# Batch 0's gate and value products: three float32r passes in the last six steps

## Chip, cores and metric

The kernel runs on 1 core of one Trainium2 chip. The metric is the device time of one execution in microseconds (us); lower is better. A core has TensorE (PE, matmuls), VectorE (DVE), ScalarE (ACT), GpSimd (POOL) and SyncE (SP). SP and ACT issue the transfers (DMA) of this kernel. Each engine works through its own list of instructions in the order in which they were written, and semaphores join the lists.

## The reference

Attention in both directions between a sequence `x` and a small `state`, then a gated feed-forward layer, then a second one:

```
scores = (x @ state.T) / sqrt(D);  a  = softmax(scores);  xread = a @ state
scores2 = (state @ x.T) / sqrt(D); a2 = softmax(scores2); sread = a2 @ x
x = concat([xread, sread], axis=2), heads side by side     # 8 batches x 544 rows, 512 columns
g = x @ w_gate;  silu = g * (1 / (1 + exp(-g)));  val = x @ w_val
x = (silu * val) @ w_out                                   # d_ff = 1536
h = x @ w_in2;   g = h * (1 / (1 + exp(-1.702 * h)))
x = g @ w_out2                                             # d_ff = 2048
```

Eight batches, 8 heads, 512 sequence rows, 32 state rows, head width 64.

## The kernel before

**Stages.** The first feed-forward layer runs batch by batch: batch 0 first, then batches 1 to 6, the state rows of all batches, batch 7. The second layer follows. The change touches batch 0 alone (`i == 0` in the code), which lies between about 25 and 154 us of the trace.

**A stage.** It has twelve steps f = 0 to 11, one for each 128 columns of d_ff. In a step PE makes the gate product (`pg`), then the value product (`pv`), and then adds the step before's result `h` into four accumulators (`out1(f - 1)`, 12 float32r passes). Behind each of the three stands a *place*, written (f, 0), (f, 1) and (f, 2), at which a plan puts other work: the next batch's attention, weight work, transfers. The plan is a table by place (`BLOCK0` for batch 1's attention, `plan_weights` for the weights), and what a place holds is written to every engine's list there and then. Nothing is moved later.

**The gate and value products.** xread is not formed. `sw` holds the state times the gate and value weights: for each batch, unit u (two steps) and group of four heads g a tile of 128 x 512 (tag `xo`). A product is the sum over g = 0, 1 of `sw` times the softmax `a` of the group. In batch 0 both are whole float32, and a product is two float32 matmuls (`mm_whole`, L337). In all other batches both are kept as a high and a low float32r part, and a product is six float32r matmuls (`mm_rows`, L330 to L332): high x high, low x high, high x low, for each g.

**Batch 0's weights.** They come whole from HBM: SP loads them (`raw`), ACT takes two passes over them (L203, L204), DVE two (L212, L213), POOL one (L216), together a *decode*. Weights of `w_out` are then also split into float32r parts by ACT (L250) and POOL (L251). A *job* (`quad_job`, PE L629, two halves into two PSUM tiles `at`) multiplies a decoded tile with the states of four batches; ACT copies the first half out (L635) and DVE the second (L636), and at the next place ACT issues their store to HBM (`move`, L652). For u of 2 and more, batch 0's rows of the result are also sent by SP from the copies into `sw`'s `xo` tile (L648). The `at` tiles have two PSUM buffers, so a half of a job waits until the tile that held its buffer before has been copied out.

**Next batch.** At (9, 0) and (9, 1) ACT issues the loads of batch 1's first `sw` rows into two tiles `xf` (`fetch`, L661), and at (10, 0) and (10, 1) `cut_fetched` splits them: ACT writes the high part (L667), POOL the low part (L668). At (9, 2) batch 1's second softmax follows on ACT, with a load of its table ahead (L503); its sums stand on DVE at (10, 0) ahead of that job's copy, and the transposes of its result on PE at (10, 1) (L540).

**Softmax tiles.** `a` of even batches lies in pool `ae`, of odd ones in `ao`.

Of the kernel before, what the change touches and what calls it, by code (L numbers as in the profile page):

```python
# [8 lines left out]
F32 = mybir.dt.float32  # L9
F32R = mybir.dt.float32r  # L10
U32 = mybir.dt.uint32
ACTF = mybir.ActivationFunctionType
ALU = mybir.AluOpType
# [61 lines left out]
def kernel(  # L75
# [24 lines left out]
    B, H, S, D = x.shape  # L100
    NS = state.shape[2]
    DM = H * D
    FF1 = w_gate.shape[1]
    FF2 = w2_in.shape[1]
    P = 128
    KD = DM // P
    F1 = FF1 // P
    U1 = F1 // 2
# [7 lines left out]
    v, a, pe, pool_e, sy = nc.vector, nc.scalar, nc.tensor, nc.gpsimd, nc.sync  # L116
# [4 lines left out]
    work = ctx.enter_context(tc.tile_pool(name="work", bufs=2))  # L121
# [7 lines left out]
    ao = ctx.enter_context(tc.tile_pool(name="odd", bufs=1, side="right"))  # L129
    ae = late.enter_context(tc.tile_pool(name="even", bufs=1, side="right"))  # L130
# [5 lines left out]
    def f32(t):  # L136
        return t.bitcast(F32)
# [147 lines left out]
    def need_whole(key):  # L285
        while pos["done"] <= where[key]:
            before = pos["done"], pos["begun"]
            whole_slot()
            assert before != (pos["done"], pos["begun"]), key
# [44 lines left out]
    def mm_whole(ps, pairs):  # L334

        for k, (w, x_) in enumerate(pairs):
            pe.matmul(ps, w, x_, start=k == 0, stop=k == len(pairs) - 1)  # L337
# [14 lines left out]
    def at():  # L352
        if extra:
            extra.append(extra.pop(0))
            if extra[0] != "at":
                return psa.tile([P, 512], F32, name="at", tag=extra[0])
        return pst.tile([P, 512], F32, name="at", tag="at")
# [43 lines left out]
    class Group:  # L401
# [118 lines left out]
            v.transpose(out=self.aT, in_=self.sp)  # L520

        def a_tile(self):
            return (ae, ao)[self.b % 2].tile([P, 2, S], F32R, name="a", tag=f"a{self.g}")

        def back_full(self):
            self.a = self.a_tile()
# [77 lines left out]
    sw = {}  # L604
# [11 lines left out]
    moved = [[], []]  # L616
    FIRST = {0: 1, 1: 4}
    OWN = 2

    def quad_job(qd, u, k, late=False):  # L620


        if qd == 0:
            need_whole(("gv", u, k))
        w = whole[u * KD + k]
        ps = [at(), at()]
        for hl in range(2):
            r = slice(hl * 64, hl * 64 + 64)
            pe.matmul(ps[hl], quad_t[qd][r, k], w[r], start=True, stop=True)  # L629
        pos["jobs"] += 1  # L630
        if qd == 0 and not late or pos["jobs"] % 3 == 0:
            t = ap.tile([P, 2, DM], F32, name="qs", tag="qs", bufs=2)
        else:
            t = work.tile([P, 2, DM], F32, name="qs", tag="raw", bufs=RAWS)
        a.copy(t[:, 0], ps[0])  # L635
        v.tensor_copy(t[:, 1], ps[1])  # L636
        g, q = divmod(k, 2)
        skip = NS * (1 - qd)
        if q == 0:
            quads[qd, u, g] = dp.tile([4 * (P - skip), DM], F32, name=f"sw{qd}_{u}_{g}")  # L640
        rows = quads[qd, u, g].rearrange("(q h p) m -> q p h m", q=2, h=2)
        moved[qd].append((rows[q], t[skip:]))
        if qd == 0 and u >= OWN:
            if q == 0:
                sw[0, u, g] = x_tiles(xp, u % 2 * 2 + g, DM)
            for hl in range(2):
                r = slice(q * 64 + hl * NS, q * 64 + hl * NS + NS)
                sy.dma_start(f32(sw[0, u, g][0][r]), t[:NS, hl])  # L648

    def move():  # L650
        for to, t in moved.pop(0):
# [3 lines left out]
    fetched = {}  # L655
# [7 lines left out]
    def cut_fetched(b, u, g, home=None):  # L663
        t = fetched.pop((b, u, g))
        pl, tag = home or (xp, f"x{u % 2 * 2 + g}")
        x_ = pl.tile([P, 2, DM], F32R, name="xo", tag=tag)
        a.copy(x_[:, 0], t)  # L667
        pool_e.tensor_tensor(x_[:, 1], t, f32(x_[:, 0]), op=ALU.subtract)  # L668
        sw[b, u, g] = x_[:, 0], x_[:, 1]

    def job_places(b):

        if b == 0:
            own = [-2, 0, 1, 2]
            first = [(n, 0, k) for k, n in enumerate((0, 1, 2, 3))]
            last = [(n, 1, k) for k, n in enumerate((28, 30, 32, 34))]
            return [(n, 0, u, k) for n, u, k in first + last] + [
                (6 * (u - 1) + own[k], 0, u, k) for u in range(OWN, U1) for k in range(KD)
            ]
        if b < 4:  # L680
            return [(n, 1, *divmod(8 * (b - 1) + j, KD)) for j, n in enumerate((3, 6, 9, 15, 18, 21, 30, 33))]
        return []

    def plan_weights(plan, i):


        b = order1[i]
        nb = order1[i + 1] if i + 1 < NB1 else None
        if nb == B:
            nb = None  # L690

        def put(f, place, fn, *args):
            plan.setdefault((f, place), []).append(lambda: fn(*args))

        for n, qd, u, k in job_places(b):
            put(n // 3, n % 3, quad_job, qd, u, k, n >= 3 * F1 - 6)
        for g in range(2):
            if 0 < b < B:
                put(b == 1, g, cut_fetched, b, 1, g)
                if b == 1:  # L700
                    put(0, g + 1, fetch, b, 1, g)
                for u in range(2, U1):
                    put(2 * u - 3, g + 1, fetch, b, u, g)
                    put(2 * u - 2 + (b == B - 1), g + (b < B - 1), cut_fetched, b, u, g)
            if nb is not None:
                put(9, g, fetch, nb, 0, g)
                put(10, g, cut_fetched, nb, 0, g, (ae, f"a{g}") if b == B else None)
                if nb > 1:
                    put(11, g, fetch, nb, 1, g)

    def mm_state(ps, b, f, t):

        c = slice(t * 2 * P + f % 2 * P, t * 2 * P + f % 2 * P + P)
        pairs = []
        if b == 0:
            mm_whole(ps, [(f32(sw[b, f // 2, g][0])[:, c], f32(groups[b, g].a[:, 0])) for g in range(2)])
            return
        for g in range(2):
            wh, wl = sw[b, f // 2, g]
            at_ = groups[b, g].a  # L720
            pairs.append((wh[:, c], wl[:, c], at_[:, 0], at_[:, 1]))
        mm_rows(ps, pairs)

# [5 lines left out]
    groups = {}  # L729
# [34 lines left out]
    def add_gv(u, k):  # L764
        r, c = slice(k * P, (k + 1) * P), slice(u * 2 * P, (u + 1) * 2 * P)
        add(("gv", u, k), (w_gate[r, c], w_val[r, c]), "place")

    for u in range(OWN):
        for k in range(KD):
            add_gv(u, k)  # L770
    for f in range(F1):
        if f // 2 + OWN < U1:
            for k in range(2):
                add_gv(f // 2 + OWN, f % 2 * 2 + k)
        add(("o", 0, f), src_out(w_out, f), "place", w1o)
# [24 lines left out]
    def x_tiles(pl, k, N):  # L800
        t = pl.tile([P, 2, S], F32R, name="xo", tag=f"x{k}")
        return t[:, 0, :N], t[:, 1, :N]
# [98 lines left out]
    for i, blk in enumerate(order1):  # L901
# [69 lines left out]
        for f in range(F1):  # L971
# [8 lines left out]
            run(f, 0)  # L980
            if i == 0 and f % 2 == 1 and f // 2 + 1 < OWN:
                state_weights(f // 2 + 1, 1)
# [348 lines left out]
```

## Time and profile before

| | us |
|---|---|
| median of 3 runs | 1491.13 |
| lowest and highest run | 1490.16 and 1491.84 |
| the profiled execution | 1492.28 |
| its span, first to last instruction | 1490.5 |
| PE busy in the span | 1467.6 (98%) |
| DVE, ACT, POOL busy | 915.6, 684.2, 396.1 |
| batch 0's steps 6 to 11 in the trace | 95.30 to 154.36 |

A row of a timeline gives the start of an instruction, its busy time, the engine, the line, the operation with its tiles (out<-in), its shape, and how many records were merged. A bracket at the end tells how long the engine had been idle before it, and what released it. A float32 matmul leaves two records. Busy times of matmuls overlap, so the length of a piece of PE's work is read from its start to the start of what follows it.

### The profile page before, as it was taken

Reading aid. Unit: us, or ns where it says so; the run is one execution under the profiler, and the core shown is the slowest. Engines: PE = TensorE matmul, PEld = TensorE weight load, DVE = VectorE, ACT = ScalarE, POOL = GpSimd, SP = SyncE. Lnnn points to the kernel's source line nnn. Section 1 sums busy time; section 2 is a strip of 40 time slices with the busy share of each in tenths; the row PEclk is TensorE's granted clock in tenths of the full one; section 3 lists DMA queues with packets and bytes.
Section 4 is the critical chain, followed back from the end, with each engine's and each line's share of the span. In section 5 each row is a group of like instructions: output and inputs, shape, how many; then the busy total and the mean of one; then the engine's idle time right before and its main releaser. Section 6 shows DMA issues by size and latency. Waiting matters only on the chain.

```text
span 1490.5 us, 21226 instructions
## 1 busy us (share of the span) xinstructions
PE 1467.6 (98%) x7688; PEld 1193.8 (80%) x7688; DVE 915.6 (61%) x1600; ACT 684.2 (46%) x1247; POOL 396.1 (27%) x325
## 2 busy tenths in 40 slices
PE   7999999999999999999999999999999999999998
PEld 4445677777787777898788889999999999999997
DVE  7985565656678787943344335656565665656554
ACT  6766554555566666654444333333333232323322
POOL 2665221222234445477646330000000000000000
PEclk9999999999999999999999999999999999999999
DMA  7975433333365656425657746565654646574653
GB/s 217 292 248 159 133 99 110 108 125 105 126 189 172 197 170 190 130 100 171 207 189 270 261 147 211 180 232 174 209 198 170 240 159 240 178 240 165 207 183 128
DMA packets 138480, 269.30 MB, mean 181 GB/s; under 512 B 46728, under 2 KB 57992, under 8 KB 138376
## 3 DMA queue, kind: packets, MB, share of 16 engines
q1 hardware_dynamic: 114680, 223.64, 45.5%
q10 hardware_dynamic: 23696, 44.31, 8.9%
q8 instruction: 61, 1.00, 0.3%
q14 instruction: 43, 0.35, 0.1%
HBM read 202.11 MB, written 63.70 MB: 178 GB/s over the span
## 4 chain that ended last, share of the span: by engine, by line
PE 84%; DMA 5%; DVE 4%; ACT 3%; issue 2%; POOL 1%; SPq 0%; ACTq 0%; DVEq 0%; POOLq 0%
PE acc L340 8%; PE acc L341 8%; PE acc L342 8%; PE acc L952 5%; PE acc L954 5%; PE gv L330 5%; PE acc L953 5%; PE gv L331 4%; PE gv L332 4%; DMA xf<-sw 4%; PE gv L1232 4%; PE gv L1231 4%; PE gv L1230 4%; PE at L629 4%; PE at L1230 3%; PE at L1231 3%
## 5 line engine op out<-in xcount | busy, mean ns | idle before, releaser
L798 DVE TENSOR_TENSOR h<-sg,h 128x512 fp32r<-128x512 f32 (+1 forms) x240 | 193.5, 806 | 129.8 <-ACT h L797 128.2
L797 ACT CAST h<-sg 128x512 fp32r<-128x512 f32 (+1 forms) x251 | 149.8, 597 | 170.4 <-DVE sg L1264 80.2
L340 PE MATMUL acc<-wo,h 128*128 128x512 f32 x512 | 200.6, 392 | 0.0
L341 PE MATMUL acc<-wo,h 128*128 128x512 f32 x512 | 200.6, 392 | 0.0
L342 PE MATMUL acc<-wo,h 128*128 128x512 f32 x512 | 199.2, 389 | 0.0
L1254 ACT ACTIVATE sg<-wt 128x512 f32<-128x512 f32 x56 | 35.4, 632 | 299.5 <-DVE wt L1252 299.5
L668 POOL TENSOR_TENSOR xo<-xf,xo 128x512 fp32r<-128x512 f32 x84 | 110.9, 1325 | 231.9 <-ACT xo L667 216.5
L952 PE MATMUL acc<-h,wu 128*128 128x512 f32 (+1 forms) x428 | 165.9, 388 | 0.1
L954 PE MATMUL acc<-h,wu 128*128 128x512 f32 (+1 forms) x428 | 163.8, 383 | 2.0 <-DVE h L798 2.0
L953 PE MATMUL acc<-h,wu 128*128 128x512 f32 (+1 forms) x428 | 163.4, 382 | 0.0
L330 PE MATMUL gv<-a,xo 128*128 128x512 f32 x336 | 137.3, 409 | 0.0
L331 PE MATMUL gv<-a,xo 128*128 128x512 f32 x336 | 133.9, 399 | 0.6 <-POOL xo L668 0.5
L332 PE MATMUL gv<-a,xo 128*128 128x512 f32 x336 | 133.0, 396 | 0.0
L992 DVE TENSOR_TENSOR sg<-gv,sg 128x512 f32<-128x512 f32 (+1 forms) x107 | 70.5, 659 | 83.1 <-PE gv L332 50.7
L342 PEld LDWEIGHTS acc<-wo,h 128*128 128x128 f32 x512 | 96.2, 188 | 20.8
L340 PEld LDWEIGHTS acc<-wo,h 128*128 128x128 f32 x512 | 96.6, 189 | 17.1
L341 PEld LDWEIGHTS acc<-wo,h 128*128 128x128 f32 x512 | 96.6, 189 | 15.8
L1252 DVE TENSOR_TENSOR wt<-wt,gv 128x256 f32<-128x256 f32 x56 | 23.6, 421 | 136.4 <-PE gv L1232 136.4
L952 PEld LDWEIGHTS acc<-h,wu 128*128 128x128 f32 x428 | 80.9, 189 | 22.1 <-issue 6.1
L977 ACT ACTIVATE sg<-gv 128x512 f32<-128x512 f32 (+1 forms) x108 | 61.5, 570 | 80.1 <-PE gv L332 77.0
L954 PEld LDWEIGHTS acc<-h,wu 128*128 128x128 f32 x428 | 80.9, 189 | 21.1 <-DVE h L798 5.5
L1232 PE MATMUL gv<-xo,wu 128*128 128x256 f32 x336 | 95.4, 284 | 0.0
(178 smaller groups left out, 3438.6 us busy)
## 6 DMA issues: line engine op xcount, KB each, us to landing
wo<-w2b SPq DMA_DIRECT2D x128, 512.0 KB
wc<-w2c SPq DMA_DIRECT2D x84, 512.0 KB
xf<-sw ACTq DMA_DIRECT2D x84, 256.0 KB
raw<-in_moe_w_out_dram SPq DMA_DIRECT2D x28, 512.0 KB
sw<-qs ACTq DMA_DIRECT2D x24, 512.0 KB
sw<-qs ACTq DMA_DIRECT2D x24, 384.0 KB
xn<-in_x_dram SPq DMA_DIRECT2D x16, 512.0 KB
y<-ev SPq DMA_DIRECT2D x16, 512.0 KB
```

Of the source, the lines that this page charges most:

```text
L330: pe.matmul(ps, wh, xh, start=k == 0, stop=False)
L331: pe.matmul(ps, wl, xh, start=False, stop=False)
L332: pe.matmul(ps, wh, xl, start=False, stop=k == len(pairs) - 1)
L340: pe.matmul(ps, lh, rh, start=first, stop=False)
L341: pe.matmul(ps, lh, rl, start=False, stop=False)
L342: pe.matmul(ps, ll, rh, start=False, stop=last)
L797: a.copy(h_, src)
L798: eng.tensor_tensor(l_, src, f32(h_), op=ALU.subtract)
L952: pe.matmul(ps, w[:, 0, c], h[:, 0, :N], start=f == 0, stop=False)
L953: pe.matmul(ps, w[:, 1, c], h[:, 0, :N], start=False, stop=False)
L954: pe.matmul(ps, w[:, 0, c], h[:, 1, :N], start=False, stop=f == F1 - 1)
L1232: pe.matmul(ps, w[:, 0, c], x_[:, 1, kt], start=False, stop=kt == 1)
```

## The change

`OWN3 = 3` is new. Batch 0's products of units 3, 4 and 5, which are the steps 6 to 11, go through `mm_rows`; units 0 to 2 stay with `mm_whole`. For that:

- `a` of batch 0 is written into `ao`, and `cut_own` splits it at (4, 0) for g = 0 and at (4, 2) for g = 1 into a tile of `ae`: ACT the high part, DVE the low part.
- Batch 0's rows of units 3 to 5 go by the same transfers into a tile `xf`, and `cut_fetched` splits them into `xo` at (5, 0), (5, 1), (7, 0), (7, 1), (9, 0) and (9, 1).

```
 def a_tile(self):
-    return (ae, ao)[self.b % 2].tile(...)
+    return (ae, ao)[self.b % 2 or not self.b].tile(...)
...
+OWN3 = 3
...
 if qd == 0 and u >= OWN:
-    if q == 0:
+    if q == 0 and u < OWN3:
         sw[0, u, g] = x_tiles(xp, u % 2 * 2 + g, DM)
+    elif q == 0:
+        fetched[0, u, g] = work.tile([P, DM], F32, name="xf", tag="xf", bufs=2)
+    to = fetched[0, u, g] if u >= OWN3 else f32(sw[0, u, g][0])
     for hl in range(2):
...
-        sy.dma_start(f32(sw[0, u, g][0][r]), t[:NS, hl])
+        sy.dma_start(to[r], t[:NS, hl])
...
+def cut_own(g):
+    t = f32(groups[0, g].a[:, 0])
+    own[g] = a_ = ae.tile([P, 2, S], F32R, name="a", tag=f"a{g}")
+    a.copy(a_[:, 0], t)
+    v.tensor_tensor(a_[:, 1], t, f32(a_[:, 0]), op=ALU.subtract)
...
 for g in range(2):
+    if b == 0:
+        put(4, 2 * g, cut_own, g)
+        for u in range(OWN3, U1):
+            put(2 * u - 1, g, cut_fetched, b, u, g)
...
-if b == 0:
+if b == 0 and f // 2 < OWN3:
     mm_whole(...)
...
-    at_ = groups[b, g].a
+    at_ = own[g] if b == 0 else groups[b, g].a
```

On ACT around places (9, 0) to (9, 2) of batch 0, where ST is the scores of batch 1's second group, xf_1148 and xf_1173 are the two fetched tiles, and ACT_TABLE_LOAD stands ahead of the softmax, before:

```order
L462 COPY ST_1146<-at_1143 128x512 [waits PE_49]
L661 DMA xf_1148<-sw0_0_0_373 128x1x512
L250 CAST wu_1153<-wt_1121 128x512 [waits Pool_49]
L635 COPY qs_1169<-at_1165 128x512 [waits DMAHW6_49,DMAHW7_49,DMAHW0_49,PE_49]
L661 DMA xf_1173<-sw0_0_1_440 128x1x512
L797 CAST h_1156<-sg_1140 128x512 [waits DVE_49]
L203 ACTIVATE wt_1189<-raw_1042 128x512 [waits DMAHW2_49]
L204 ACTIVATE raw_1042<-raw_1042 128x512
L652 DMA sw0_1_0_1172<-qs_1169 96x2x512 [waits DVE_49,Activation_49]
L503 ACT_TABLE_LOAD
```

The same stretch of ACT after the change; xf_1056 and xf_1143 are batch 0's rows of unit 5:

```order
L462 COPY ST_1192<-at_1189 128x512 [waits PE_49]
L671 CAST xo_1194<-xf_1056 128x512
L665 DMA xf_1197<-sw0_0_0_373 128x1x512 [waits Pool_49]
L250 CAST wu_1206<-wt_1163 128x512
L636 COPY qs_1222<-at_1218 128x512 [waits DMAHW6_49,DMAHW7_49,DMAHW0_49,PE_49]
L671 CAST xo_1226<-xf_1143 128x512 [waits DMAHW2_49,DMAHW1_49]
L665 DMA xf_1229<-sw0_0_1_440 128x1x512 [waits Pool_49]
L813 CAST h_1209<-sg_1186 128x512 [waits DVE_49]
L203 ACTIVATE wt_1245<-raw_1076 128x512
L204 ACTIVATE raw_1076<-raw_1076 128x512
L656 DMA sw0_1_0_1225<-qs_1222 96x2x512 [waits DVE_49]
L503 ACT_TABLE_LOAD
```

Two casts (L671) came in, and both fetches now wait for POOL: a fetched tile takes the buffer that POOL's split of batch 0's rows reads. The high part is cast from the same buffer just ahead of each.

On DVE around places (4, 0) and (4, 1), from the copy of job (4, 0) to the copy of job (4, 1), before:

```order
L636 COPY qs_742<-at_739 128x512
L212 TENSOR_SCALAR wf_711<-wf_711 128x512
L213 SCALAR_TENSOR_TENSOR wf_711<-raw_644,wf_711 128x512
L992 TENSOR_TENSOR sg_736<-gv_747,sg_736 128x512
L511 TENSOR_REDUCE sq_677<-sp_676 128x16
```

The same stretch of DVE after:

```order
L637 COPY qs_742<-at_739 128x512
L681 TENSOR_TENSOR a_747<-a_304,a_747 128x512
L212 TENSOR_SCALAR wf_711<-wf_711 128x512
L213 SCALAR_TENSOR_TENSOR wf_711<-raw_644,wf_711 128x512
L1008 TENSOR_TENSOR sg_736<-gv_750,sg_736 128x512
L511 TENSOR_REDUCE sq_677<-sp_676 128x16
```

The subtraction for the low part of `a` (L681) stands directly behind the job's copy and ahead of the decode; it waits for ACT's cast of the high part.

## Rows read from the trace of the kernel before

**Rows 1.** Page, busy time: engine, us, share of the span, instructions.

```profile
PE 1467.6 (98%) x7688; PEld 1193.8 (80%) x7688; DVE 915.6 (61%) x1600; ACT 684.2 (46%) x1247; POOL 396.1 (27%) x325
```

**Rows 2.** Timeline of PE, steps 6 and 7 of batch 0: float32 products among their neighbours.

```profile
99.53 1.98 PE L337 MATMUL gv<-a,xo 128*128 128x512 f32 x4
101.44 1.13 PE L629 MATMUL at<-wf,qt 64*128 64x512 f32 x4
...
106.51 1.98 PE L337 MATMUL gv<-a,xo 128*128 128x512 f32 x4
108.33 0.60 PE L432 MATMUL at<-ident,xn 128*128 128x128 f32 x4
108.77 1.88 PE L337 MATMUL gv<-a,xo 128*128 128x512 f32 x4
110.58 1.13 PE L629 MATMUL at<-wf,qt 64*128 64x512 f32 x4
```

**Rows 3.** Timeline of PE in batch 1: two six-pass products, first pass and successor.

```profile
160.73 0.48 PE L330 MATMUL gv<-a,xo 128*128 128x512 f32 x1
...
162.30 1.20 PE L629 MATMUL at<-wf,qt 64*128 64x512 f32 x4
163.43 0.50 PE L330 MATMUL gv<-a,xo 128*128 128x512 f32 x1
...
164.94 0.40 PE L452 MATMUL at<-xth,stc 128*128 128x512 f32 x1
```

**Rows 4.** Timeline of DVE in batch 0.

```profile
76.13 0.90 DVE L212 TENSOR_SCALAR wf<-wf 128x512 uint32<-128x512 uint32 x1
...
85.73 0.69 DVE L636 COPY qs<-at 128x512 f32<-128x512 f32 x1 [2.32 <-PE at L629]
...
91.14 1.48 DVE L534 TENSOR_TENSOR a<-aT,a 128x512 fp32r<-128x512 f32 x1
...
97.19 1.17 DVE L575 TENSOR_SCALAR srd<-at,sm 32x64 f32<-32x64 f32 x4
...
138.07 0.69 DVE L636 COPY qs<-at 128x512 f32<-128x512 f32 x1
```

**Rows 5.** Timeline of ACT in batch 0.

```profile
78.32 0.58 ACT L635 COPY qs<-at 128x512 f32<-128x512 f32 x1
...
116.50 0.62 ACT L250 CAST wu<-wt 128x512 fp32r<-128x512 f32 x1 [0.78 <-POOL wt L216]
...
118.63 0.58 ACT L635 COPY qs<-at 128x512 f32<-128x512 f32 x1
...
128.54 0.58 ACT L462 COPY ST<-at 128x512 f32<-128x512 f32 x1 [1.12 <-PE at L337]
128.55 1.11 ACTq L661 DMA_DIRECT2D xf<-sw  x1
...
131.31 0.59 ACT L635 COPY qs<-at 128x512 f32<-128x512 f32 x1 [0.99 <-PE at L629]
131.32 0.53 ACTq L661 DMA_DIRECT2D xf<-sw  x1
...
134.28 1.28 ACT L503 ACT_TABLE_LOAD   x1 [0.64 <-DVE qs L636]
```

**Rows 6.** Timeline of POOL in batch 0: the low part of a fetched tile.

```profile
139.90 1.30 POOL L668 TENSOR_TENSOR xo<-xf,xo 128x512 fp32r<-128x512 f32 x1 [2.96 <-ACT xo L667]
```

**Rows 7.** Timeline of PE in batch 0: halves of jobs, and the transposes at (10, 1).

```profile
98.51 1.09 PE L629 MATMUL at<-wf,qt 64*128 64x512 f32 x2 [0.28 <-DVE srd L575]
...
119.72 1.13 PE L629 MATMUL at<-wf,qt 64*128 64x512 f32 x4
...
138.90 0.63 PE L540 MATMUL at<-ident,e 128*128 128x128 f32 x4
```

**Rows 8.** Windows: stretch, its length, PE, PEld, DVE, ACT, POOL busy, granted clock, DMA share, GB/s.

```profile
78.00:80.00 2.00, 1.05 (x2) 0.29 (x2) 1.97 (x4) 2.00 (x5) 1.31 (x2) 1.00 0.13 45
80.00:84.53 4.53, 4.53 (x13) 3.31 (x12) 3.31 (x6) 2.19 (x5) 2.48 (x3) 0.62 0.89 250
```

More of the change, by code (lines that the diff above doesn't have):

```diff
@@ L522, in a_tile @@
         def a_tile(self):
-            return (ae, ao)[self.b % 2].tile([P, 2, S], F32R, name="a", tag=f"a{self.g}")
+            return (ae, ao)[self.b % 2 or not self.b].tile([P, 2, S], F32R, name="a", tag=f"a{self.g}")
         def back_full(self):
@@ L669, in cut_fetched @@
         sw[b, u, g] = x_[:, 0], x_[:, 1]
+    own = {}
+    def cut_own(g):
[3 more added lines that the diff above has]
+        v.tensor_tensor(a_[:, 1], t, f32(a_[:, 0]), op=ALU.subtract)
     def job_places(b):
```

## The prediction

> **What bounds the kernel now.** The page's busy times come first: PE works 98% of the span [rows 1], so a stage ends when PE has done its list, and the question is what PE's list gets shorter by and where PE begins to wait. In batch 0 the second question is open, because there all engines decode weights beside the products. The timelines of PE, DVE, ACT and POOL between 70 and 155 us answer it place by place. The reader is to see two things in them. A product of batch 0 is read from its start to the start of what follows [rows 2], a six-pass product in batch 1 likewise [rows 3]. And some pieces of PE's list already start at the moment at which a copy on DVE or ACT ends: the second half of job (6, 0) 0.28 us after PE was free [rows 7], and the transposes at (10, 1), which start at 138.90, when the copy that DVE began at 138.07 and that took 0.69 has just ended [rows 4, 7]. At such a place a shorter product before it gains nothing, and anything put in front of the copy costs PE its full length.
>
> **The products.** Twelve change. A float32 product takes 1.91 us between two jobs (99.53 to 101.44), 1.82 after a job and ahead of transposes, 1.81 between transposes and a job [rows 2]. Six float32r passes take 1.57 between transposes and a job, and 1.51 after a job when other full-height work follows [rows 3]; between two jobs I estimate 1.59. Six products (gate of 6, 8, 10; value of 7, 9, 11) save 1.81 - 1.57 = 0.24 each, the value products of 6 and 8 save 0.32, the other four 0.31: 1.44 + 0.64 + 1.24 = 3.3 us, or 0.22%. In order: 1.67 up to the end of value product 8, 0.31 in gate product 9, 0.79 from there to the transposes at (10, 1), 0.55 in step 11.
>
> The Trainium skill, "FP8 and Floating Point Precision", section "TensorE Precision Notes", counts four passes for true FP32. By it a product would go from eight passes to six, and at the 0.235 us a pass of [rows 3] twelve products would give an estimated 5.6 us; the rows show 3.3, since passes that follow a half-height job or stand ahead of one cost more, and the sum goes by the rows.
>
> **What is added.** ACT gets eight casts (two of `a`, six of rows), 0.5 to 0.6 us each; POOL six subtractions of 1.30 [rows 6]; DVE two, each between 0.69 (the length of its plain passes over 128x512 [rows 4]) and 1.48 (the same operation for batch 1's softmax, [rows 4]). DVE's are free only where DVE waits anyway. The transfers are as many and as large as before, into `xf` in place of `xo`; a later fill waits for POOL's split of the tile before, with weight loads behind it on SP, but that split lies a place earlier, and I cost it at nothing. The new home of `a` makes batch 1's cast at (5, 1) wait for a product that PE has then done: nothing.
>
> **First wait, job (6, 0).** In step 4 DVE's subtraction stands ahead of the decode that began at 76.13 [rows 4]. It waits for a cast that on ACT can only follow the job's copy (78.32, 0.58 [rows 5]), so until about 79.4. Everything behind it on DVE starts some 3.9 us later. I estimate that DVE makes this good by 85.73, with the 2.32 us in which it waited for PE there and with passes that ran long beside POOL, as the one at 76.13, and now run alone [rows 4]. PE's job (4, 2) is then not held up. The second subtraction at (4, 2) finds no such gap: ACT's cast, 0.4 us of waiting and 0.65 of work leave DVE about 1.05 us late until step 6, where POOL's extra splits also run against it. The state sums that began at 97.19 [rows 4] then end at about 99.4 in place of 98.36. PE arrives 0.24 earlier and its second half starts at about 99.55 in place of 98.51 [rows 7]. So PE is 1.0 us late there (bounds: 0.2, if DVE catches up, and 1.6, if the second subtraction also takes 1.48).
>
> **Second wait, job (8, 1).** POOL does 2 x 1.30 us more in step 7 [rows 6]; I estimate that between 0.7 and 1.5 of it falls into time in which POOL stood idle. ACT's cast at 116.50 already waits for POOL there (0.78), and the copy at 118.63 stands 2.13 us behind it [rows 5]. POOL 1.1 to 1.9 us later moves that copy to 119.7 to 120.5, with its end at 120.3 to 121.0; the second half of job (8, 1), which before could start half a us after 119.72 [rows 7], waits for it. The products of value 6 to value 8 have by then won back 1.43, which goes into this wait or the first. I take PE 0.3 us late after this job, with ends of -1.67 (no wait at all) and +0.8.
>
> **Third wait, the transposes at (10, 1).** This is the largest term. I count from ACT's copy of the scores, S = 128.54 [rows 5], which follows PE. Before, the fetch is issued at once (1.11 us), the table load starts at 134.28, S + 5.74, and ACT has 0.99 and 0.64 us of slack ahead [rows 5]. Now: cast of unit 5's rows, done at S + 1.1; POOL's split 1.30, S + 2.4; only then may ACT issue the fetch (0.53 to 1.11 us [rows 5]), S + 3.0 to 3.5, and everything behind it on ACT has waited. Cast of `w_out`, job copy and second cast end at S + 4.6 to 5.2, while POOL subtracts the `w_out` tile until S + 4.9 to 5.4 and the second rows until S + 6.2 to 6.8. The second fetch waits for that. Then `h` (0.5) and the decode pair (1.1) follow, and the table load starts at S + 8.4 to 9.0, 2.7 to 3.3 us late. Behind it stand the exponentials, DVE's sums, DVE's job copy and PE's transposes, which had no slack. So from S to the transposes PE takes 10.36 + 3.0 us, and the 0.79 us that three products save in between are swallowed.
>
> **The clock.** By then PE has stood idle some 3 + 0.8 = 3.8 us. In the windows, PE was busy 1.05 of 2.00 us around (4, 1) at the full clock, and the clock was 0.62 in the next 4.53 us, that is for most of them at the lower of its two levels, 1.2 in place of 2.4 GHz [rows 8]. Those 12 passes took 4.53 us in place of 12 x 0.235 = 2.82 [rows 3, 8]: up to 1.7 lost. An idle time three times as long should bring the same to `out1(9)`: 1.6 us, with ends of 0 and 2.4.
>
> **Sum.** +0.3 after step 8, -0.31 for gate product 9, +3.0 at the transposes, -0.55 for step 11, +1.6 for the clock: +4.0 us. The profiled execution took 1492.28 (span 1490.5 and 1.78 around it), so 1496.3 against it; it stood 1.15 above the median, so against the median 1495.1.
>
> **Rivals.** (1) *The clock holds*, all else the same: +2.4, 1493.5. For it: the idle piece of 0.28 at 98.51 left no mark. Against: the fall behind (4, 1). (2) *The fetches do not hold ACT*, because POOL is ahead and the splits end by the time ACT gets there. Then ACT's 1.1 us of extra casts fit into its 0.99 + 0.64 of slack, the transposes stay at S + 10.36, and the sum is +0.3 - 0.31 - 0.55 = -0.6, 1490.5: not slower. It decides at a table load by S + 5.8, which needs POOL's second split by about S + 4; the `w_out` subtraction alone ends at S + 4.9. (3) *No engine but PE matters*: all 3.3 us come, 1487.8. Against it stand the two places at which PE starts as a copy ends. (4) *The clock falls at (6, 0) too*, where PE waits about 2 us between two jobs, as it did at (4, 1): another 1.6, 1496.7.
>
> **How the numbers follow.** A measurement of this kernel tells about 0.2%, 3.0 us, from no change. Chances: forecast 0.45, (1) 0.20, (2) 0.15, (3) 0.10, (4) 0.10. Faster needs (3): 0.10. (1) and (2) lie within 0.2%: 0.35. The forecast and (4) are slower by more: 0.55. The range leaves out (3) and the far end of the rest: from 1489.5 (case (2) with the first two waits 1 us smaller) to 1498.5 (case (4) with the waits at their upper ends).
>
> **What would show it.** In the changed kernel's trace: products of steps 6 to 11 of 1.51 to 1.59 us; the DVE subtraction of (4, 0) starting about 79.4 with an idle time ahead that ended on ACT; job (6, 0)'s second half waiting about 2 us for DVE's state sums; ACT's fetch issues at (9, 0) and (9, 1) behind POOL's splits; the table load at S + 8.4 to 9.0; a PE idle time of 3 to 4 us ahead of the transposes at (10, 1), released by DVE's copy; and a lower granted clock right behind it. It is wrong if the table load comes at S + 6 or earlier, or if PE shows no idle time of over 1 us between 95 and 145 us.

## The result, and the profile after

The changed kernel takes **1506.6 us** (median of 5 executions, 1502.08 to 1507.94) against 1491.13. The ratio on record is 1.0089, with a 95% interval of 1.0075 to 1.0103; it is not the quotient of the two medians, which is 1.0104. The change is slower by some 0.9 to 1.0%, where the prediction had 0.27% and a range that ended at 1498.5. The profiled execution, 1502.08 us with a span of 1500.0, is the shortest of the five. Lines of code from L629 on moved by 1 to 16 (a job is now L630, its copies are L636 and L637, the fetch L665, the split of rows L671 and L672, that of the softmax L680 and L681); in the variants further down they move by a few more.

On the page PE is busy 2.3 us *longer* than in [rows 1], though its list got shorter:

```profile
PE 1469.9 (98%) x7712; PEld 1202.0 (80%) x7712; DVE 922.9 (62%) x1602; ACT 688.0 (46%) x1255; POOL 407.0 (27%) x331
```

PE's timeline shows products near the forecast, and three waits at the places named in the prediction; the rows answer to [rows 2] and [rows 7]:

```profile
102.08 2.04 PE L630 MATMUL at<-wf,qt 64*128 64x512 f32 x2 [3.66 <-DVE srd L575]
...
112.24 0.49 PE L330 MATMUL gv<-a,xo 128*128 128x512 f32 x1
...
113.74 0.60 PE L432 MATMUL at<-ident,xn 128*128 128x128 f32 x4
114.09 0.48 PE L330 MATMUL gv<-a,xo 128*128 128x512 f32 x1
...
115.66 0.70 PE L630 MATMUL at<-wf,qt 64*128 64x512 f32 x2
...
127.59 1.72 PE L630 MATMUL at<-wf,qt 64*128 64x512 f32 x2 [1.43 <-ACT qs L636]
134.66 1.18 PE L630 MATMUL at<-wf,qt 64*128 64x512 f32 x4
...
153.54 0.63 PE L540 MATMUL at<-ident,e 128*128 128x128 f32 x4 [3.54 <-ACT sg L993]
```

Gate product 7 is 1.50 us long (112.24 to 113.74), value product 7 1.57. But job (6, 0) starts its second half 3.57 us later than before, job (8, 2) at 134.66 in place of 123.75, and the transposes at 153.54 in place of 138.90: 14.64 us. The profile names ACT's `sg` (L993, which ended at 153.47) as what released the transposes, where the prediction had DVE's copy (ended at 153.39); both stand behind ACT's table load. Two smaller waits were in no step of the prediction: the gate products of steps 8 and 10 stop for POOL's low part (L672), 0.60 us up to 121.72 and 1.11 us up to 146.60. Each is followed by a longer wait for another engine (1.43 and 3.54 us), so they seem to have cost nothing of their own.

The windows (start and end, length, busy us of PE, PEld, DVE, ACT and POOL, granted clock, DMA share, GB/s) show why the matmuls behind the first two waits are long, and that behind the third they are not:

```profile
102.00:107.00 5.00, 4.92 (x10) 2.41 (x10) 1.81 (x3) 1.68 (x4) 1.94 (x2) 0.50 0.44 134
...
127.00:135.00 8.00, 7.41 (x16) 4.43 (x18) 3.00 (x4) 4.07 (x8) 6.24 (x5) 0.57 0.45 131
153.00:157.00 4.00, 3.46 (x18) 2.70 (x20) 1.70 (x3) 4.00 (x8) 2.46 (x2) 1.00 0.52 138
```

0.50 is the lower of the clock's two levels (1.2 GHz) for the whole stretch. PE's "busy" time grows with it. The kernel before has 1.00 in the first two of these:

```profile
102.00:107.00 5.00, 5.00 (x21) 2.77 (x18) 2.69 (x5) 2.62 (x5) 3.94 (x3) 1.00 0.90 274
127.00:135.00 8.00, 8.00 (x27) 4.24 (x26) 4.55 (x9) 4.67 (x8) 3.75 (x3) 1.00 0.38 117
```

DVE in steps 4 to 6, answering to [rows 4]: the first subtraction stands idle 3.24 us for ACT's cast, and the state sums that release job (6, 0) begin 3.58 us late.

```profile
79.36 0.69 DVE L681 TENSOR_TENSOR a<-a 128x512 fp32r<-128x512 f32 x1 [3.24 <-ACT a L680]
...
86.17 0.69 DVE L637 COPY qs<-at 128x512 f32<-128x512 f32 x1 [0.15 <-PE at L630]
86.78 1.16 DVE L681 TENSOR_TENSOR a<-a 128x512 fp32r<-128x512 f32 x1
...
96.72 1.65 DVE L213 SCALAR_TENSOR_TENSOR wt<-raw,wt 128x512 uint32<-128x512 uint32 x1
...
100.77 1.17 DVE L575 TENSOR_SCALAR srd<-at,sm 32x64 f32<-32x64 f32 x4
```

From its copy at (4, 2) to the state sums DVE took 14.60 us (86.17 to 100.77), where the kernel before took 11.46 (85.73 to 97.19). Of the 3.14 us more, 1.07 are the second subtraction, counted up to the next pass, and about 2.1 are decode passes that ran longer beside POOL: two of L213 (at 88.30 and 96.72) with 1.65 us in place of 0.69, and one L212 with 1.11 in place of 0.88.

ACT in steps 7 and 8, and then from S (its copy of the scores, 139.19), answering to [rows 5]:

```profile
124.84 0.62 ACT L250 CAST wu<-wt 128x512 fp32r<-128x512 f32 x1 [3.92 <-POOL wt L216]
...
126.95 0.58 ACT L636 COPY qs<-at 128x512 f32<-128x512 f32 x1
...
139.19 0.59 ACT L462 COPY ST<-at 128x512 f32<-128x512 f32 x1 [1.12 <-PE at L337]
...
141.68 1.11 ACTq L665 DMA_DIRECT2D xf<-sw  x1
...
146.58 0.53 ACTq L665 DMA_DIRECT2D xf<-sw  x1
147.15 0.62 ACT L813 CAST h<-sg 128x512 fp32r<-128x512 f32 x1 [2.69 <-POOL xo L672]
...
148.93 1.28 ACT L503 ACT_TABLE_LOAD   x1
```

The fetches wait for POOL's splits, and the table load starts at S + 9.74 (before S + 5.74). The wait for POOL's decode at 124.84 has grown from 0.78 to 3.92 us.

Batch 1's list begins 14.1 us late (its first transposes at 200.07 in place of 185.96), and yet the span grew by only 9.5. Nearly all of the difference lies in one later stretch, in the stages of batches 4 to 6: from the transposes (L540) at 467.76 to those at 621.35 the kernel before took 153.59 us, the changed one 148.45. That stretch is taken up below.

### The profile page after: what moved, and what is told of

It reads as the page before. It is cut to its first block, busy times and chain, and to the rows that moved or that the text cites. A ratio compares the mean times of both kernels' runs of the same rounds, so it can differ in the third digit from the quotient of the medians.

```text
span 1500.0 us, 21287 instructions
## 1 busy us (share of the span) xinstructions
PE 1469.9 (98%) x7712; PEld 1202.0 (80%) x7712; DVE 922.9 (62%) x1602; ACT 688.0 (46%) x1255; POOL 407.0 (27%) x331
## 4 chain that ended last, share of the span: by engine, by line
PE 84%; DMA 4%; DVE 3%; ACT 3%; issue 2%; POOL 2%; SPq 1%; ACTq 0%; DVEq 0%; POOLq 0%
PE acc L340 8%; PE acc L341 8%; PE acc L342 8%; PE gv L330 5%; PE acc L970 5%; PE gv L331 5%; PE acc L968 5%; PE acc L969 5%; PE gv L332 5%; PE gv L1248 4%; PE gv L1247 4%; PE gv L1246 4%; PE at L630 3%; PE at L1246 3%; PE at L1247 3%; PE at L1248 3%
## 5 line engine op out<-in xcount | busy, mean ns | idle before, releaser
L672 POOL TENSOR_TENSOR xo<-xf,xo 128x512 fp32r<-128x512 f32 x90 | 122.4, 1364 | 229.7 <-ACT xo L671 210.3
L330 PE MATMUL gv<-a,xo 128*128 128x512 f32 x360 | 148.8, 413 | 0.0
L331 PE MATMUL gv<-a,xo 128*128 128x512 f32 x360 | 144.1, 400 | 2.9 <-POOL xo L672 2.9
L332 PE MATMUL gv<-a,xo 128*128 128x512 f32 x360 | 142.9, 397 | 0.0
L341 PEld LDWEIGHTS acc<-wo,h 128*128 128x128 f32 x512 | 96.6, 189 | 15.8
L330 PEld LDWEIGHTS gv<-a,xo 128*128 128x128 f32 x360 | 67.9, 189 | 36.9 <-issue 23.7
L993 ACT ACTIVATE sg<-gv 128x512 f32<-128x512 f32 (+1 forms) x108 | 61.6, 570 | 78.2 <-PE gv L332 77.8
```

Source lines behind the costliest of these rows:

```text
L330: pe.matmul(ps, wh, xh, start=k == 0, stop=False)
L331: pe.matmul(ps, wl, xh, start=False, stop=False)
L332: pe.matmul(ps, wh, xl, start=False, stop=k == len(pairs) - 1)
L341: pe.matmul(ps, lh, rl, start=False, stop=False)
```

## The experiments

Each row is one program; positions are PE's start times in its profile. "Late stretch" is the one just named. "Next" is the first transposes behind batch 0's stage. Each ratio is taken against executions of the kernel before that ran beside that variant, not against 1491.13.

| | median, us | ratio to before [95%] | job (6, 0), second half | job (8, 2) | (10, 1) | next | late stretch |
|---|---|---|---|---|---|---|---|
| before | 1491.13 | | 98.51 | 123.75 | 138.90 | 185.96 | 153.59 |
| before, again (e11) | 1492.14 | 1.0004 [0.9991, 1.0018] | 97.97 | 123.21 | 138.36 | 187.18 | 149.67 |
| after | 1506.60 | 1.0089 [1.0075, 1.0103] | 102.08 | 134.66 | 153.54 | 200.07 | 148.45 |
| after, again (e12) | 1509.46 | 1.0116 [1.0086, 1.0147] | 103.53 | 135.31 | 154.13 | 202.94 | 152.45 |
| e1 products | 1487.27 | 0.9976 [0.9966, 0.9987] | 98.27 | 124.36 | 138.86 | 185.41 | 149.24 |
| e2 softmax split | 1494.64 | 1.0034 [1.0022, 1.0047] | 100.31 | 127.23 | 142.38 | 189.43 | 150.48 |
| e3 row splits | 1503.83 | 1.0087 [1.0065, 1.0110] | 100.17 | 132.43 | 151.60 | 200.23 | 148.58 |
| e4 late fetch | 1499.31 | 1.0060 [1.0040, 1.0080] | 102.07 | 134.51 | 149.99 | 196.75 | 148.00 |
| e5 fill | 1504.90 | 1.0082 [1.0061, 1.0104] | 102.35 | 129.45 | 148.27 | 197.96 | 153.56 |
| e6 unit 4 on DVE | 1503.59 | 1.0078 [1.0056, 1.0100] | 102.35 | 132.43 | 151.26 | 199.34 | 149.00 |
| e7 early casts | 1502.08 | 1.0069 [1.0054, 1.0084] | 99.59 | 129.79 | 148.63 | 196.95 | 151.16 |
| e8 all three | 1495.57 | 1.0030 [1.0018, 1.0042] | 99.98 | 129.13 | 144.70 | 191.06 | 149.80 |
| e9 unit 5 only | 1491.36 | 0.9995 [0.9979, 1.0011] | 98.32 | 123.55 | 139.71 | 185.97 | 149.92 |
| e10 units 4 and 5 | 1493.42 | 1.0013 [1.0001, 1.0026] | 98.44 | 125.82 | 141.29 | 187.86 | 151.68 |

Where an expectation says "six passes" of batch 0's products, the whole float32 products are meant. In e2 the whole products of the last six steps read the rounded half of the softmax, in e3 that of the rows.

**The late stretch first, since it limits what a total can tell.**

```
the kernel before, and the changed kernel, once more
```

> The kernel before once more, for a second profile. Between the transposes at 467.8 and 621.4 its first profile took 153.6 us, that of the changed kernel 148.4 us, and those of the other variants 148.0 to 153.6. Theory (that stretch differs from one execution to the next, whatever the change): this profile gives another value than 153.6, anywhere from 148 to 154, while all up to 467.8 comes at the same times within 0.3 us. Rival (the changed kernel really gains 5 us there): 153.6 again.

> The changed kernel once more, for a second profile. Theory (the stretch from the transposes at 482.1 to those at 630.6 differs between executions): about 153 us in place of 148.4, which the median of 1506.6 against the profiled 1502.1 asks for, with stage 0 as in the first profile (first transposes of the next stage at 200.1). Rival: 148.4 again, and the difference lies elsewhere.

The late stretch took 149.67 us in the second profile of before and 152.45 in that of after: the order turned round. It lies between 148.0 and 153.6 in all fourteen profiles and follows no part of the change. PE's waits there differ from execution to execution (5.2 us in the first profile of before, 2.1 in the second, 1.1 in the first of after), and totals are good to some 3 us: the median of the changed kernel moved by 2.9 us between its two rounds. Why the waits differ is left open.

The expectation for before missed elsewhere: the times up to 467.8 were not repeated within 0.3 us. The fall of the clock behind job (4, 1), [rows 8], did not come, and job (6, 0) came 0.54 us sooner. Then the clock fell behind job (11, 1), where the first profile had 1.00, and the next stage came at 187.18: with nothing changed, 48.82 us from the transposes at (10, 1) in place of 47.06. In the changed kernel, too, the second profile lacked the fall behind (4, 1) and had one behind the transposes, which the first had not; the next stage came at 202.94, not at 200.1. Its three waits came again (3.61, 1.43 and 3.54 us), at places 0.6 to 2.1 us later. The windows are two of before again and one of after again:

```profile
80.00:90.00 10.00, 9.98 (x34) 4.90 (x34) 9.06 (x14) 7.91 (x15) 6.78 (x5) 1.00 0.85 255
150.00:160.00 10.00, 10.00 (x37) 7.45 (x38) 2.06 (x5) 2.45 (x6) 1.27 (x1) 0.83 0.15 45
```

```profile
150.00:160.00 10.00, 6.46 (x23) 4.16 (x21) 6.22 (x10) 7.58 (x13) 6.16 (x5) 0.83 0.48 127
```

From here on the positions in batch 0 carry the argument, and totals only where they agree. A difference of under some 2 us in a position may be one between two executions; where an engine's way between two of its own instructions is given, it repeats better.

**e1: the products alone.**

```
 def cut_own(g):
     a.copy(a_[:, 0], t)
-    v.tensor_tensor(a_[:, 1], ...)
...
-        put(2 * u - 1, g, cut_fetched, b, u, g)
...
+    if b == 0:
+        pairs.append((own[g][:, 0][:, c], own[g][:, 0][:, c], own[g][:, 0], own[g][:, 0]))
```

> The three-pass products alone. Left out: the splits of the rows and the subtraction of the softmax (every operand of the six steps is the softmax's rounded half, so only the two ACT casts of 0.6 us are left of the added work). Theory (the splits' work on DVE, POOL and ACT makes the three waits): the waits at job (6,0), job (8,1) and the transposes (10,1) are as in the kernel before (under 0.5 us at (6,0)), the products take 1.50 to 1.60 us, and the time is 1.5 to 3.3 us below before: about 1488.5. Rival (shorter products alone turn PE's slack into waits, or drop the clock): no gain or a loss, 1491 to 1495, with a clock below 0.9 in one of the windows 100:110, 120:130, 130:140.

Its median is 3.3 us below before, but within batch 0 nearly nothing of that is seen. PE's timeline of e1, and a window behind job (6, 0):

```profile
98.27 1.09 PE L630 MATMUL at<-wf,qt 64*128 64x512 f32 x2 [0.91 <-DVE srd L575]
...
120.33 1.13 PE L630 MATMUL at<-wf,qt 64*128 64x512 f32 x4 [0.88 <-ACT qs L636]
...
138.86 0.63 PE L540 MATMUL at<-ident,e 128*128 128x128 f32 x4 [0.63 <-ACT sg L992]
```

```profile
97.00:102.00 5.00, 4.09 (x11) 2.01 (x10) 2.89 (x7) 2.90 (x6) 2.88 (x3) 0.76 0.66 202
```

At each of the three places PE now arrives earlier and waits longer, and the transposes start 0.04 us from where they did; job (8, 2) even comes 0.6 later. Only step 11 is kept: 0.55 us at the next stage. The rival's clock came too: it fell behind the wait of 0.91 us at job (6, 0) (0.76 in the window, where the kernel before has 1.00), while the fall behind job (4, 1) stayed out, so e1 doesn't separate the products from the clock. Both halves of the expectation held in part: without the splits the large waits are gone (0.91 us at (6, 0), though, not under 0.5), and the products' gain up to step 10 goes into small waits and a fall of the clock. The rest of the 3.3 us lies in the late stretch (149.24 in place of 153.59) or in the clock's falls, and cannot be put down to the products.

**e2 and e3: each split alone.**

```
# e2: rows as before, all products whole
-        put(2 * u - 1, g, cut_fetched, b, u, g)
# e3: rows split, softmax as before, all products whole
-        put(4, 2 * g, cut_own, g)
```

> Only the softmax's split at step 4 (two casts on ACT, two subtractions on DVE); the rows are not split and all products stay in six passes. Theory 1 (the wait at (6,0) comes from DVE's own two added passes): second half of job (6,0) waits about 3 us or more, the clock falls behind it, +4 to +6 us: 1495 to 1497. Theory 2 (most of the wait comes from DVE passes that run long beside POOL's added splits): the wait at (6,0) is 1.0 to 1.6 us, +1 to +3 us: 1492 to 1494.

> Only the rows of units 3 to 5 are split (ACT casts, POOL subtractions, SP's transfers into other tiles); the softmax is not split and all products stay in six passes. Theory 1 (DVE's two passes make the wait at (6,0)): wait at (6,0) under 1 us, waits at (8,1) and (10,1) stay, +5 us: 1496. Theory 2 (POOL's splits stretch DVE's passes): 2 to 2.5 us of wait at (6,0) with a fall of the clock, and the other two waits: +8 to +11 us: 1499 to 1502.

At job (6, 0) the softmax's split alone costs 1.80 us (100.31 against 98.51), the rows' splits alone 1.66, and both together 3.57: two causes of about equal size, which nearly add up. Positions alone would be a weak ground for this (e2's profile lacked the fall behind job (4, 1), as before's second did, and against that one the softmax's share is 2.34). DVE's way from its copy at (4, 2) to the state sums bears it out: 11.46 and 11.44 us in the two profiles of before, 12.70 in e2, 13.17 in e3, and 14.60 in both profiles of after. Theory 2 held for both waits (1.40 and 1.99 us), while both totals lay above the expected ones. How the rows' splits work is seen on DVE, which has no instruction more in e3. Two decode passes ahead of the state sums, in the kernel before and then in e3, with the POOL passes beside them in e3:

```profile
94.10 0.69 DVE L213 SCALAR_TENSOR_TENSOR wt<-raw,wt 128x512 uint32<-128x512 uint32 x1
94.71 0.42 DVE L212 TENSOR_SCALAR wf<-wf 128x512 uint32<-128x512 uint32 x1
```

```profile
93.75 1.64 DVE L213 SCALAR_TENSOR_TENSOR wt<-raw,wt 128x512 uint32<-128x512 uint32 x1
95.31 1.48 DVE L212 TENSOR_SCALAR wf<-wf 128x512 uint32<-128x512 uint32 x1
```

```profile
93.39 1.45 POOL L672 TENSOR_TENSOR xo<-xf,xo 128x512 fp32r<-128x512 f32 x1
94.81 1.71 POOL L813 TENSOR_TENSOR h<-sg,h 128x512 fp32r<-128x512 f32 x1
```

0.69 became 1.64 and 0.42 became 1.48, while POOL worked without a break. Each of the two DVE passes began while a POOL pass ran, and ended 0.55 and 0.27 us after that POOL pass did. DVE's copies out of PSUM keep their 0.68. The Trainium skill, "SBUF — State Buffer", section "SBUF: two separate sides", says that DVE (with two SBUF inputs, or in a mode that uses two ports) and GpSimd share one pair of SBUF ports, and that whichever starts first holds it for its whole instruction while the other stands still; the ends of these passes agree with it. That L212, with one source, uses such a mode is not shown here.

The other two waits are the rows' work: e3 has both (2.09 us at (8, 1), 3.99 at the transposes), e2 has neither. In PE's positions e3 is as late as the whole change (200.23 and 200.07); it has the longer whole products, and a fall behind the transposes (0.83 in 150:160) that the first profile of the change has not.

**e4: the third wait.**

```
-put(9, g, fetch, nb, 0, g)
-put(10, g, cut_fetched, nb, 0, g, ...)
+put(9 + (b == 0), g + (b == 0), fetch, nb, 0, g)
+put(10 + (b == 0), g, cut_fetched, nb, 0, g, ...)
```

> The changed kernel with batch 1's two fetches and splits a step later ((10,1), (10,2) and (11,0), (11,1) in place of (9,0), (9,1), (10,0), (10,1)). Theory (ACT stands in its fetches until POOL has split batch 0's rows): the table load comes at S + 6.5 to 7.0 in place of S + 9.74, the idle time ahead of the transposes falls from 3.5 to under 1 us, and the time is 2.5 to 3.5 us below the changed kernel: 1503 against 1506.6. Rival (POOL's splits hold `h` and the xo tiles anyway): the table load stays past S + 8.5 and the time within 1 us.

ACT from S on, and the transposes, in e4:

```profile
139.00 0.59 ACT L462 COPY ST<-at 128x512 f32<-128x512 f32 x1 [1.12 <-PE at L337]
...
144.42 1.28 ACT L503 ACT_TABLE_LOAD   x1 [0.22 <-ACT raw L204]
```

```profile
149.99 0.63 PE L540 MATMUL at<-ident,e 128*128 128x128 f32 x4 [1.56 <-ACT wu L250]
```

The table load comes at S + 5.42, earlier than before's S + 5.74, with both added casts ahead of it. The transposes come at S + 10.99 (after S + 14.35, before S + 10.36), and the next stage 3.3 us earlier. The fetches in ACT's list were the whole third wait but for 0.6 us. That ACT itself had room for the casts was right. Two numbers of the expectation missed: PE still stands idle 1.56 us ahead of the transposes, not under 1, and the median came 7.3 us below the changed kernel's, of which the positions show 3.3.

**e5: the clock.**

```
+again = {(4, 1): 4, (5, 2): 2}.get((u, k), 1) if qd == hl == 0 else 1
+for _ in range(again):
     pe.matmul(ps[hl], quad_t[qd][r, k], w[r], start=True, stop=True)
```

> The changed kernel with PE kept at work in its two waits: the first half of job (6, 0) is computed four times and that of job (8, 1) twice, into the same bank (1.1 us a time, 3 more and 1 more, less than the waits of 3.66 and 1.43 us). Theory (TensorE's clock falls because PE stands idle there): the second halves start where they did (102.1 and about 125), the granted clock is 1.00 in the windows 100:110 and 130:140, the stretch from job (6, 0) to (6, 1) shrinks by about 1.9 us and that from job (8, 1) to (8, 2) by about 3.5 us; the time is 4 to 5.5 us below the changed kernel. Rival (the clock falls for another reason, or the time comes back as waits): clock below 0.9 in those windows, time within 1.5 us of the changed kernel.

The same windows as above, in e5, with the two stretches behind its transposes:

```profile
102.00:107.00 5.00, 4.65 (x16) 2.48 (x17) 3.44 (x7) 2.84 (x6) 2.66 (x3) 1.00 0.60 183
...
127.00:135.00 8.00, 8.00 (x31) 4.92 (x29) 2.92 (x5) 4.75 (x9) 6.14 (x5) 1.00 0.64 186
```

```profile
150.00:160.00 10.00, 10.00 (x36) 6.53 (x34) 3.31 (x5) 2.94 (x6) 4.70 (x4) 0.89 0.58 146
160.00:170.00 10.00, 9.32 (x32) 6.85 (x32) 2.60 (x7) 2.39 (x5) 1.28 (x1) 0.83 0.15 43
```

With PE at work in its waits the second half of job (6, 0) starts where it did (102.35), and the clock stays at 1.00. To job (6, 1) it takes 2.62 us in place of 4.83; counted by positions, (6, 1) moves from 106.91 to 104.97 (1.94 us) and (8, 2) from 134.66 to 129.45. Of those 5.2 us some 3.0 are new behind job (8, 0) (9.24 in place of 12.27 us from there to (8, 2)). So PE's idle time does bring the clock down at these places, at a price of about 2 and 3 us. But then the clock fell twice behind the transposes, where it had not fallen (0.89 and 0.83 in the last two windows): the next stage starts only 2.1 us earlier, and the median is 1.7 below. A price saved at one wait was paid at the next; both theories were half right.

**e6, e7, e8: the causes one by one, and together.**

```
# e6: unit 4's low parts
-pool_e.tensor_tensor(x_[:, 1], t, ...)
+(v if (b, u) == (0, 4) else pool_e).tensor_tensor(x_[:, 1], t, ...)
# e7: casts at (2, 0), (2, 1), both subtractions at (4, 1)
-put(4, 2 * g, cut_own, g)
+put(2, g, cut_own, g)
+put(4, 1, low_own, g)
# e8: e4, e6 and e7
```

> The changed kernel with unit 4's two low parts subtracted on DVE in place of POOL. Theory (the wait at job (8, 1) is POOL's decode pass L216, which stands behind unit 4's splits): the wait at (8, 1) falls under 0.5 us, the clock stays at 1.00 in 130:140, job (8, 2) comes 4 to 5 us earlier than 134.66, and the time is 3 to 5 us below the changed kernel. Rival (DVE's two more passes hold the same chain up): the wait stays over 1 us and the time within 1.5 us.

> The changed kernel with the softmax's casts on ACT at (2, 0) and (2, 1) and both subtractions on DVE at (4, 1), where DVE stood idle for 2.32 us in the kernel before. Theory (DVE stands idle 3.2 us ahead of the first subtraction for ACT's cast, with decode passes queued behind it; that, not the two passes, is the softmax's share): the idle time ahead of the subtraction is under 0.2 us, job (6, 0)'s second half starts at about 100.2 in place of 102.08 (the place of the rows alone), and the time is 1.5 to 2 us below the changed kernel. Rival (two passes more on a full DVE are the cost wherever they stand): it starts at 101.5 or later, time within 1 us.

> The late fetch, unit 4's low parts on DVE and the early casts together. Theory (three separate causes, which add up): 3.7 + 4 + 1.8 us below the changed kernel, about 1496 to 1498; what stays is unit 3's splits on POOL beside DVE's decode (1.7 us of wait at (6, 0) and the fall of the clock behind it). Rival (what is gained at one wait is lost at the next): 1499 or more, as the late fetch alone.

In e6 job (8, 1) no longer waits for POOL's decode, but for DVE, whose copy stands behind the passes put there. PE's timeline of e6:

```profile
125.36 1.09 PE L630 MATMUL at<-wf,qt 64*128 64x512 f32 x2 [0.89 <-DVE qs L637]
...
126.85 1.12 PE L630 MATMUL at<-wf,qt 64*128 64x512 f32 x2 [0.39 <-ACT qs L636]
```

1.28 us of wait in place of 1.43: the rival's wait. Job (8, 2) came 2.2 us earlier, not 4 to 5, with a shorter fall of the clock (0.79 in 127:135 in place of 0.57); by the next stage 0.7 were left. The median is 3.0 us lower, as the theory had it, but the positions don't bear that out. In e7 both subtractions run as soon as DVE comes to them, in the gap of [rows 4], and the state sums come 2.5 us earlier:

```profile
81.54 1.83 DVE L684 TENSOR_TENSOR a<-a 128x512 fp32r<-128x512 f32 x2
...
98.28 1.17 DVE L575 TENSOR_SCALAR srd<-at,sm 32x64 f32<-32x64 f32 x4
```

In e7's profile the fall of the clock behind job (4, 1), [rows 8], also stayed out; e8, which has it, starts the second half at 99.98, no later than the rows' splits alone (100.17). So the two passes cost nothing where DVE has room and the cast lies ahead, against the rival. Whether the idle time of 3.2 us ahead of the first was the whole of the softmax's share, as the theory said, e7 doesn't show, for it moved the second pass as well (1.07 us in the changed kernel). The gain, 3.1 us at the next stage and 4.5 in the median, was larger than forecast. Together (e8) the three bring the next stage from 200.07 to 191.06, 9.0 us where they bring 7.1 one by one, and the time to 1495.57, 1.0030 of before: near the theory's 1496 to 1498, and not the rival's 1499. What stays is unit 3's splits on POOL (99.98 at job (6, 0)), the copy at (8, 1), and 1.65 us at the transposes.

**e9 and e10: fewer steps, with room.** Batch 0's float32 softmax moves into unused room beside the `st` tiles, so that its split can wait until engines are free.

```
-OWN3 = 3
+OWN3 = 5                       # e10: 4
...
+put(((6, 1), (6, 2))[g][0], ..., cut_own, g)    # e10: (5, 2), (6, 1)
+put(8, 2, low_own, g)                           # e10: (6, 2)
# fetches as in e4; e10: unit 4 as in e6
```

> Three passes in the last two steps only: unit 5's rows split (ACT, POOL, steps 9 and 10), the softmax cast on ACT at (6, 1) and (6, 2) and subtracted on DVE at (8, 2), where DVE stood idle (3.62 us busy of 10 in 120:130), batch 1's fetches late. Theory (each wait comes from a piece of the splits that lands on a full engine; where engines have slack it costs nothing): job (6, 0) and job (8, 1) wait as in the kernel before (0.3 and 0.5 us), transposes at S + 10.4 to 11.0, the first transposes of the next stage at 185.4 to 186.1 against 185.96, and a time within 0.2% of before (1489 to 1493), since only step 11's 0.55 us are left to win. Rival (three passes lose in any number of steps): 1494 or more.

> Three passes in the last four steps: units 4 and 5 split, unit 4's low parts on DVE, the softmax cast at (5, 2) and (6, 1) and subtracted at (6, 2), batch 1's fetches late. Theory: the wait at job (6, 0) is gone (0.3 us), job (8, 1) still waits 1.0 to 1.5 us for the copies, so the first transposes of the next stage come at 187 to 189 and the time is 1 to 4 us above before: 1492 to 1495. Rival (unit 3's splits were the whole loss): 185.4 to 186.5 and 1489 to 1492.

PE's timeline of e9, and of e10:

```profile
98.32 1.09 PE L632 MATMUL at<-wf,qt 64*128 64x512 f32 x2 [0.27 <-DVE srd L577]
...
139.71 0.63 PE L542 MATMUL at<-ident,e 128*128 128x128 f32 x4 [1.59 <-ACT wu L250]
```

```profile
120.36 1.09 PE L632 MATMUL at<-wf,qt 64*128 64x512 f32 x2 [1.28 <-DVE qs L639]
```

Both came out much as the theory had them (e9's transposes came at S + 11.4, somewhat later than forecast). With only the last two steps changed the first two waits are as before, the next stage starts at 185.97, and the time is that of before. With four steps the copies at (8, 1) cost PE about 2 us, of which 1.9 are left at the next stage. No variant with splits beats the kernel before.

## Why the prediction was right or wrong

**The sign and the places were right, the sum was a quarter of the truth.** Forecast was +4.0 us, measured +15.5 in the median (13.3 by the ratio on record), and to the next stage +14.1 in the first pair of profiles and +15.8 in the second (202.94 against 187.18). In the first pair PE loses, in order, 3.57 us up to job (6, 0), 1.90 from there to (6, 1), 0.17 to (8, 0), 5.27 to (8, 2) and 3.73 to the transposes: 14.64, of which step 11 gives 0.5 back. The prediction had PE 0.3 late after step 8; it was 10.9.

**The products: right where they stand as forecast.** Eight of the twelve, read where nothing held them up (in this kernel, e1 and e5), took 1.49 to 1.60 us, with 1.51 to 1.59 forecast. But gate 6 and value 11 took 1.67 and 1.68, and value 9 took 1.90, longer than before's 1.81: these three stand behind other float32 matmuls, and not behind transposes as the prediction had them. So the sum is nearer 2.9 than 3.3 us. The reason that the prediction gives for 3.3 in place of 5.6 us is half shown: in a six-pass product a pass next to a job takes 0.32 to 0.34 us and the others 0.23, but the whole products stand beside the same jobs, and their 1.81 to 1.91 us are 0.23 to 0.24 for each of the eight passes that it counts. That only step 11's 0.55 would survive was nearly said (0.79 "swallowed"); e1 shows that the other 1.98 go the same way.

**First wait, +1.0 forecast, +3.57 measured.** The first subtraction began at 79.36 (79.4 forecast), so DVE's idle time was seen, and the second held DVE up for 1.07 us (1.05 forecast, if as 0.4 of waiting and 0.65 of work). The step that failed is POOL's extra splits: a half-sentence, with no price on DVE. They cost it 1.9 us between (4, 2) and the state sums (14.60 us, and 12.70 in e2, which does not split the rows), and 1.66 at job (6, 0) by e3, since DVE's passes beside them ran 1.64 in place of 0.69. The trace of before had such pairs (L213 took 1.65 us at 77.06 and 0.69 at 82.72). That DVE makes the first subtraction good by 85.73 came out within 0.44 us (86.17) in the first pair of profiles, where PE was held up by the fall of the clock behind (4, 1). In the second pair, without that fall, DVE was 2.40 late there (87.62 against 85.22), and PE waited 1.01 us at job (4, 2), which the prediction had ruled out. So this step was right by luck.

**The clock at the first wait: a rival that came true.** The sum had no fall there. Rival (4) had one, with a chance of 0.10; the fall behind (6, 0) cost 1.94 by e5 (1.6 forecast).

**Second wait, +0.3 forecast.** ACT's cast waited 3.92 us for POOL, not 0.78 plus 1.1 to 1.9: POOL worked from 113.52 to 124.81 without a break, and its passes beside DVE took 1.45 to 1.77 us each, not 1.30. From job (8, 0) to (8, 2) PE took 12.27 us in place of 7.00: about 3.0 for a second fall of the clock (e5), the rest for the wait. No case of the prediction had a fall there. In the second profile that fall was shorter, and the stretch took 10.79 us.

**Third wait, +3.0 forecast, +4.0 measured.** The mechanism was right (e4 takes the wait away). POOL's second split ended later than assumed: the second fetch was issued at S + 7.39, not at 6.2 to 6.8.

**The clock behind the third wait: +1.6 forecast.** None in the first profile. In the second it fell (0.83 in 150:160), and the way from the transposes to the next stage took 48.81 us in place of 46.53. In before's second profile it fell in that window too. It cost 2.3 us in the one kernel and 1.8 in the other. The size was about right, the place is not fixed.

**What no step had:** the late stretch, 148 to 154 us by chance, which alone moves the total by more than all products.

**The range** failed for two reasons. The clock was one term at one place, while three waits of over 1.4 us are three chances for a fall, at 2 to 3 us each. And the forecast waits were too short: without the two falls (1.9 and 3.0 us) PE would still have been some 9 us late, and the range ended 7.4 us above the median of before.

## What to carry to other kernels

A split that shortens the busiest engine's work is paid for on engines that are full at that place: what counts is not the passes' sum but what stands behind them in each in-order list, above all a pass that waits there for another engine (e4 took the waiting fetches out of ACT's way, e7 put the softmax's split where DVE had room and nothing to wait for; each won back 3 us without taking one instruction away). Cost DVE's and POOL's passes at their length beside each other, and give each new wait of the matrix engine of about a microsecond or more a second price for the clock (here a fall followed waits of 0.91 us in e1, 1.43 and 3.66). Where a saving ends ahead of a place that another engine times, count it as nothing (e1).

## What the hardware showed

- A DVE pass over 128x512 with two sources (L213) took 0.69 us alone and 1.64 when it began beside a running POOL pass (e3), one with one source (L212) 0.42 and 1.48; POOL's 1.30 became up to 1.77.
- After 3.66 us of idle time the granted clock was 0.50 for 5 us; after 3.54 at the transposes it was 1.00 in one execution and 0.83 (over 10 us) in another of the same program. Taking falls away at two waits (e5) brought two behind a third. Behind the same wait of 0.68 us at job (11, 1) it fell in one execution of the kernel before and not in another, and behind 1.28 us at job (8, 1) in e10 it stayed at 1.00. What decides this stayed open.
- With nothing changed, the way of PE through a later stretch (467.8 to 621.4) took 153.59 us in one execution and 149.67 in another.
